# One store in ten of an attention gradient, cut into 120 and 8 partitions

## The chip, the cores and the metric

The kernel runs on one core of one Trainium2 chip. The metric is the device time of one execution in microseconds (us). Three executions of the kernel before took 1323.01, 1326.78 and 1328.87 us; the median is 1326.78.

## The reference

One query attends to 8192 keys, for 2 x 32 = 64 heads of 128 elements, all in bf16. The outputs are the attention's result and the gradients with respect to q, k and v, given the gradient of the result:

```
scores = einsum("bhqd,bhkd->bhqk", q, k) * D**-0.5     # B, H, Sq, Sk, D = 2, 32, 1, 8192, 128
p      = softmax(scores)
out    = einsum("bhqk,bhkd->bhqd", p, v)
# returned: out, and the gradients dq, dk, dv for a given grad_out
```

For each head, k and v (2 MB each) have to be read once, and dk and dv (2 MB each) have to be written once. Every row of dv is the softmax weight of that key times grad_out, and every row of dk is the gradient of that key's score times q. So 537 MB pass between the main memory and the chip, against a few thousand bytes for all else.

## The kernel before, in words

**Tiling.** The 8192 rows of a head are spread over the 128 partitions of the on-chip memory, 64 rows (NT) a partition, so that one partition holds 16 KB that lie in one piece in the main memory. A head's k is one tile kt (128 x 64 x 128), its v one tile vt. There are five buffers of each (UNITS). A load is one DMA of 2 MB, issued on SP's queue (line 103). Transfers of 128 partitions run on sixteen DMA engines, eight partitions to an engine, and each engine reports its own end of the transfer.

**Work on one head.** TensorE turns blocks of kt and vt (line 112, `transposes`), ScalarE or VectorE bring them out of PSUM (lines 119 and 117), and TensorE multiplies them with q and grad_out (line 135, `products`). Then follow the row maximum, the exponentials, the sums and the weights (`row_max` to `weights`). TensorE sums rows for out and dq (line 240, `weighted_rows`). At last VectorE writes the gradients over the loaded tiles themselves (line 270, `outer`): dv over vt, dk over kt. `store` (line 278) sends such a tile to the main memory, one DMA of 2 MB, also on SP's queue. With w = 0 it stores dv out of vt, with w = 1 dk out of kt. The last head alone is stored in halves.

**Order.** The order of all instructions is written out by hand. In step h of the main loop (line 304 and after) the transposes and products of head h are interleaved, in eight parts j, with the weighted rows, the gradients and the stores of head h-1. At the end of step h, load(h+3) is issued (line 343 is its call), into the buffers that head h-2 had; so it waits until both stores of head h-2 have landed. Since loads and stores go out on one queue, in order, whatever waits on SP holds up all that is behind it. Each DMA takes the next of eight semaphores in turn, and first waits for the DMA that had it before.

The lines that matter in what follows: 103 (loads), 112 (transposes), 270 (gradients), 278 (stores), 343 (the call of `load` in the loop).

Of the kernel before, what the change touches and what calls it, by code (L numbers as in the profile page):

```python
# [15 lines left out]
HC = CH // 2  # L16
QG = 4
OG = 4
UNITS = 5


@with_exitstack
def kernel(
# [11 lines left out]
    nc = tc.nc  # L35
    B, H, Sq, D = q.shape
    Sk = k.shape[2]
    P = nc.NUM_PARTITIONS
# [3 lines left out]
    assert NT * P == Sk and NT == 4 * CH and BH <= P and BH % QG == 0  # L42
    assert BH % OG == 0 and OG * 8 == 32
    NS = 2 * NT // CH
# [9 lines left out]

    pick = const.tile([P, 4, 2, OG], F32)
    idv = ident_f[:].rearrange("p (g w k j) -> p g j w k", g=4, w=2, k=OG)
    nc.vector.tensor_copy(out=pick[:], in_=idv[:, 0])
    for g in range(1, 4):
# [6 lines left out]

    kvp = ctx.enter_context(tc.tile_pool(name="kv", bufs=UNITS))
    evp = ctx.enter_context(tc.tile_pool(name="ev", bufs=5))
# [8 lines left out]
    dk_v = out_2.rearrange("b h (p n) d -> (b h) p n d", n=NT)  # L76
    dv_v = out_3.rearrange("b h (p n) d -> (b h) p n d", n=NT)
# [8 lines left out]
    wz = [  # L86
        [const.tile([P, NT // 4, 32], BF16, name=f"wz{w}{k}") for k in range(OG)]
        for w in range(2)
# [5 lines left out]
    heads = [Head() for _ in range(BH)]  # L94

    def load(h):
        x = heads[h]
        x.kv = [
            kvp.tile([P, NT, D], BF16, name="kt", tag="kt"),
            kvp.tile([P, NT, D], BF16, name="vt", tag="vt"),  # L100
        ]
        for dst, src in zip(x.kv, (k_v, v_v)):
            nc.sync.dma_start(out=dst[:], in_=src[h])  # L103
# [79 lines left out]
    def to_weights(h, w, src):  # L183
        k = h % OG
        nc.vector.tensor_copy(  # L185
            out=wz[w][k][:, :, 16 * w + 4 * k : 16 * w + 4 * k + 4],
            in_=src[:].rearrange("p (m j) -> p m j", j=4),
        )
# [44 lines left out]
    def weighted_rows(h, w, chunks):  # L233


        rows, k = heads[h].kv[1 - w], h % OG
        for c in chunks:
# [37 lines left out]
        )  # L275

    def store(h, w, a=0, b=NT):
        nc.sync.dma_start(out=(dv_v, dk_v)[w][h][:, a:b, :], in_=heads[h].kv[1 - w][:, a:b, :])  # L278

    def outer_and_store(h, w, i):  # L280

        outer(h, w, i)
        if h == BH - 1:
            if i % 2:
                store(h, w, (i - 1) * CH, (i + 1) * CH)
        elif i == NT // CH - 1:
            store(h, w)
# [13 lines left out]
    with tc.manual_schedule():  # L301
        for h in range(min(UNITS, BH)):
            load(h)
        for h in range(BH + 1):
# [4 lines left out]
            for j in range(NS):  # L309
# [31 lines left out]
                if j == 7:  # L341
                    if x and UNITS <= h + 3 < BH:
                        load(h + 3)
# [38 lines left out]
```

## Time and profile before

| What | Value |
|---|---|
| Median of three runs | 1326.78 us |
| The profiled execution: its time, its span | 1328.14 us, 1326.3 us |
| Bytes read from and written to main memory | 268.47 MB and 268.47 MB |
| 16 KB packets on SP's queue | 32512, of which the usual one takes 0.611 us |
| Granted TensorE clock, mean | 0.89 |

The span goes from the first instruction to the last. The page of the profile gives the busy time of each compute engine, then the span in forty equal slices with the mean busy share of the sixteen DMA engines (in tenths) and the GB/s that they moved, then the DMA queues with the time that their packets took as a share of sixteen engines' span, and last the DMA issues by line, with the median time from the issue to the landing, which is the last of the sixteen engines' reports. Where a view gives waits, it names who waited for whom, the total, how often, and the longest.

### The profile page before, as it was taken

What the parts mean: (1) busy time and instruction counts of PE and PEld (TensorE: products, weight loads), DVE (VectorE), ACT (ScalarE), POOL (GpSimd) and SP (SyncE); (2) the same over time, 40 slices, a digit from 0 to 9 for tenths busy, and PEclk for the clock granted to TensorE, in tenths of its full rate; (3) what the DMA queues carried; (4) which work ended last, traced back from release to release, by engine and by line L of the source; (5) the groups of instructions that cost most, each with busy time, mean ns of one, the idle gap of its engine ahead of it and who ended that gap; (6) DMA issues with size and microseconds to landing.
All of it is one profiled execution on the core that took longest, in us unless ns stands there. A gap on an engine that the chain in (4) does not pass through costs nothing.

```text
span 1326.3 us, 42070 instructions
## 1 busy us (share of the span) xinstructions
PE 1108.8 (84%) x18948; PEld 909.2 (69%) x18948; DVE 887.3 (67%) x1511; ACT 906.7 (68%) x1043; POOL 4.8 (0%) x16
## 2 busy tenths in 40 slices
PE   5999898898788887888879878798888888898883
PEld 5777777776676766766767667676766676676762
DVE  2887777676666766767657666575766666676664
ACT  5877787776766766767677676676766676676662
POOL 1000000000000000000000000000000000000000
PEclk9999999988988989989799888987988888888886
DMA  9999999999999999999999999999999999999985
GB/s 396 422 427 426 428 426 428 427 427 429 426 426 419 421 413 417 419 412 415 412 410 405 406 403 400 405 405 401 400 397 409 395 406 403 397 401 392 410 371 242
DMA packets 37652, 539.64 MB, mean 407 GB/s; under 512 B 4448, under 2 KB 4448, under 8 KB 4448
## 3 DMA queue, kind: packets, MB, share of 16 engines
q1 hardware_dynamic: 37152, 536.89, 98.2%
q8 instruction: 148, 2.42, 0.6%
q14 instruction: 32, 0.26, 0.0%
q10 hardware_dynamic: 320, 0.07, 0.0%
HBM read 268.47 MB, written 268.47 MB: 405 GB/s over the span
## 4 chain that ended last, share of the span: by engine, by line
DMA 63%; PE 21%; ACT 8%; DVE 4%; issue 1%; SPq 1%; ACTq 0%; DVEq 0%
DMA out_dram<-kt 36%; DMA kt<-in_k_dram 27%; PE tp L112 13%; ACT ev L119 8%; PE acc L240 5%; DVE ev L117 3%; PE sm L135 2%; DMA nat<-in_grad_out_dram 1%; PE dp L205 1%; DVE kt L270 1%; PE dp L135 1%; SPq L103 0%; SPq L278 0%; PE sm L169 0%; DVE vt L270 0%
## 5 line engine op out<-in xcount | busy, mean ns | idle before, releaser
L119 ACT CAST ev<-tp 128x1024 bf16<-128x1024 f32 x896 | 879.2, 1026 | 379.3 <-PE tp L112 364.4
L112 PE MATMUL tp<-ident_bf,kt 128*128 128x128 bf16 x4096 | 379.9, 247 | 119.2 <-DMA kt<-in_k_dram 115.1
L112 PEld LDWEIGHTS <-kt 128*128 128x128 bf16 x4096 | 280.2, 110 | 256.0 <-issue 133.8
L117 DVE CAST ev<-tp 128x1024 bf16<-128x1024 f32 x128 | 156.7, 1224 | 298.5 <-PE tp L112 293.5
L112 PE MATMUL tp<-ident_bf,vt 128*128 128x128 bf16 x4096 | 313.4, 219 | 48.2 <-ACT ev L119 38.0
L135 PEld LDWEIGHTS <-ev 128*128 128x128 bf16 x8192 | 333.0, 100 | 2.2 <-issue 0.2
L112 PEld LDWEIGHTS <-vt 128*128 128x128 bf16 x4096 | 259.1, 98 | 81.6 <-issue 73.1
L270 DVE TENSOR_TENSOR kt<-qd,dS 128x2048 bf16<-128x2048 bf16 x256 | 310.0, 1212 | 0.0
L270 DVE TENSOR_TENSOR vt<-qd,P 128x2048 bf16<-128x2048 bf16 x256 | 295.8, 1217 | 0.0
L135 PE MATMUL dp<-doT_all,ev 128*128 128x1 bf16 x4096 | 180.3, 165 | 0.1
L135 PE MATMUL sm<-qT_all,ev 128*128 128x1 bf16 x4096 | 178.0, 164 | 0.0
L240 PE MATMUL acc<-vt,wz 128*32 128x512 bf16 x1024 | 127.8, 489 | 4.7 <-DVE wz L185 4.5
L240 PE MATMUL acc<-kt,wz 128*32 128x512 bf16 x1024 | 106.1, 407 | 0.5 <-DVE wz L185 0.5
L240 PEld LDWEIGHTS <-wz 128*32 128x32 bf16 x2048 | 53.7, 95 | 16.3 <-DVE wz L185 6.8
L159 DVE TENSOR_REDUCE mp<-sm 128x1 f32<-128x64 f32 x64 | 14.4, 225 | 55.1 <-PE sm L135 55.1
L205 PE MATMUL dp<-ld,ones_f 128*128 128x2 f32 x128 | 27.8, 287 | 10.4 <-DVE ld L192 9.5
L205 PEld LDWEIGHTS dp<-ld,ones_f 128*128 128x128 f32 x128 | 23.3, 228 | 17.8 <-DVE ld L192 17.5
L210 DVE RECIPROCAL rl_all<-dp 128x1 f32<-128x1 f32 x64 | 10.7, 168 | 34.7 <-PE dp L205 34.7
L153 ACT CAST qd<-pb 128x1024 bf16<-128x1024 f32 x16 | 16.2, 1012 | 12.3 <-PE pb L145 12.3
L169 PE MATMUL sm<-gm,ones_f 1*128 1x1 f32 x128 | 24.2, 256 | 0.0
L169 PEld LDWEIGHTS sm<-gm,ones_f 1*128 1x128 f32 x128 | 18.7, 182 | 6.6
L174 ACT ACTIVATE E_f<-sm,negm 128x64 f32<-128x64 f32 x64 | 23.1, 361 | 0.0
(40 smaller groups left out, 263.2 us busy)
## 6 DMA issues: line engine op xcount, KB each, us to landing
kt<-in_k_dram SPq DMA_DIRECT2D x64, 2048.0 KB, 25.4
vt<-in_v_dram SPq DMA_DIRECT2D x64, 2048.0 KB, 30.2
out_dram<-vt SPq DMA_DIRECT2D x63, 2048.0 KB, 34.8
out_dram<-kt SPq DMA_DIRECT2D x63, 2048.0 KB, 39.5
out_dram<-vt SPq DMA_DIRECT2D x2, 1024.0 KB, 12.0
out_dram<-kt SPq DMA_DIRECT2D x2, 1024.0 KB, 12.1
out_dram<-rows ACTq DMA_DIRECT2D x2, 16.0 KB, 5.8
nat<-in_q_dram ACTq DMA_DIRECT2D x1, 16.0 KB, 8.1
```

The source lines that it names most:

```text
L112: nc.tensor.matmul(tp[:, i, :], lhsT=x.kv[w][:, n, :], rhs=ident_bf[:], start=True, stop=True)
L117: nc.vector.tensor_copy(out=ev[:], in_=tp[:])
L119: nc.scalar.copy(out=ev[:], in_=tp[:])
L135: nc.tensor.matmul((x.dp if w else x.sm)[:, n : n + 1], lhsT=ev[:, i, :], rhs=col, start=True, stop=True,)
L153: nc.scalar.copy(out=qd[:], in_=pb[:])
L159: nc.vector.reduce_max(out=x.mp[:], in_=x.sm[:, 0:NT], axis=AX.X)
L169: nc.tensor.matmul(mb, lhsT=ones_f[0:1, :], rhs=x.gm[:], start=True, stop=True)
L174: nc.scalar.activation(out=x.E[:], in_=x.sm[:, 0:NT], func=ACT.Exp, bias=negm[:], scale=scale, accum_out=x.ld[:, 0:1],)
L205: nc.tensor.matmul(x.lsum, lhsT=ones_f[:], rhs=x.ld[:], start=True, stop=True)
L210: nc.vector.reciprocal(out=rl, in_=x.lsum[:, 0:1])
L240: nc.tensor.matmul(acc[32 * g : 32 * g + 32, :], lhsT=wz[w][k][:, n // 4, :], rhs=rows[:, n : n + 4, :].rearrange("p n d -> p (n d)"), sta ...
L270: nc.vector.tensor_tensor(out=x.kv[1 - w][:, n : n + CH, :].rearrange("p n (d t) -> p n d t", t=2), in0=row.unsqueeze(1).to_broadcast([P, ...
```

## The change

In one call of `store` out of ten, the 128 partitions go as two DMAs: partitions 0 to 119, which is eight partitions for each of fifteen DMA engines, and partitions 120 to 127, one for each of the first eight. Counting stores as 2h + w, the ones chosen are 9, 19, ... 119, twelve of 128, and all of them are stores of dk (w = 1, heads 4, 9, ... 59). The same bytes are stored in the same places. Nothing else is changed; the order of the work stays as it was.

```diff
+FEW = 120
+SKIP = 10
 UNITS = 5
...
     def store(h, w, a=0, b=NT):
-        nc.sync.dma_start(out=(dv_v, dk_v)[w][h][:, a:b, :], in_=heads[h].kv[1 - w][:, a:b, :])
+        cuts = (0, FEW, P) if (2 * h + w) % SKIP == SKIP - 1 else (0, P)
+        for lo, hi in zip(cuts, cuts[1:]):
+            nc.sync.dma_start(
+                out=(dv_v, dk_v)[w][h][lo:hi, a:b, :], in_=heads[h].kv[1 - w][lo:hi, a:b, :]
+            )
```

## The prediction

> **What bounds the kernel now.** I read the totals first. The span is 1326.3 us, the execution itself 1328.14 us (1.84 us lie around the span), and the median of the three runs is 1326.78 us, so a sum made against this execution is lowered by 1.36 us to stand beside the median.
>
> ```profile
> span 1326.3 us, 42070 instructions
> PE 1108.8 (84%) x18948; PEld 909.2 (69%) x18948; DVE 887.3 (67%) x1511; ACT 906.7 (68%) x1043; POOL 4.8 (0%) x16
> ...
> DMA  9999999999999999999999999999999999999985
> GB/s 396 422 427 426 428 426 428 427 427 429 426 426 419 421 413 417 419 412 415 412 410 405 406 403 400 405 405 401 400 397 409 395 406 403 397 401 392 410 371 242
> ...
> q1 hardware_dynamic: 37152, 536.89, 98.2%
> q8 instruction: 148, 2.42, 0.6%
> ```
>
> No compute engine is full; the DMA engines are, in every slice but the last two. Yet what they move falls from 427 to about 400 GB/s while their busy share stays full. So "busy" does not mean "at full rate", and next I asked for the stretches before and after that fall.
>
> ```profile
> 60.00:400.00 340.00, 298.57 (x5362) 245.71 (x5360) 250.01 (x426) 256.10 (x296) 0.00 (x0) 0.95 1.01 427
> 800.00:1260.00 460.00, 392.46 (x6494) 321.81 (x6494) 302.92 (x518) 310.80 (x357) 0.00 (x0) 0.85 1.00 401
> ```
>
> Columns are length, PE, PEld, DVE, ACT, POOL, granted clock, DMA share, GB/s. One head moves 8 MB (two loads, two stores): 19.7 us at 427 GB/s, 20.9 at 401. PE's work for a head is 17.3 us in the first stretch and about 17.8 in the second, so PE is not the limit in either. Then the waits of SP's queue:
>
> ```profile
> SPq L103 <- DMA out_dram<-kt: 943.2, 55, 19.5
> SPq L278 <- DVE vt L270: 136.9, 14, 22.1
> ```
>
> A load (line 103) waits until the last store of the head that held its buffers has landed. The DMA issues say how long that is:
>
> ```profile
> kt<-in_k_dram SPq DMA_DIRECT2D x64, 2048.0 KB, 25.4
> vt<-in_v_dram SPq DMA_DIRECT2D x64, 2048.0 KB, 30.2
> out_dram<-vt SPq DMA_DIRECT2D x63, 2048.0 KB, 34.8
> out_dram<-kt SPq DMA_DIRECT2D x63, 2048.0 KB, 39.5
> ```
>
> A transfer alone needs about 5 us; the last store of a head lands 39.5 us after its issue. Who is late? The trace has sixteen completion events for each transfer, one from each DMA engine. For some dk stores, in us from the span's start:
>
> ```
> head  issued    first     8th      15th     16th    16th-15th
>   1     63.51    71.68    72.67    73.70    73.94    0.2
>  14    299.89   324.48   330.39   332.28   339.36    7.1
>  30    627.74   648.74   650.83   652.35   667.21   14.9
>  56   1172.61  1193.32  1194.28  1196.17  1212.74   16.6
> ```
>
> **One DMA engine is late.** Fifteen end within 3 us of each other, the sixteenth 17 us behind, and each next load is issued less than 0.1 us after that sixteenth event. Between 70 and 400 us, before its lag is full, the mean time from one transfer to the next is, ranked by engine: five at 4.87 us, two at 4.90, eight at 4.96 to 4.97 (4.965 below), one at 5.108. In stores the late one needs 5.37 us against 4.93 for the others, in loads 4.86, no more than they. Once it is 18 us behind the first of the others, its lag stands still and the other fifteen slow down, in their loads alone: 4.93 us a load early, 5.55 after 800 us. The late engine sets the pace; the others queue behind a buffer that only it still holds. Extra bytes are not the reason: in the last 8 us it works alone and a 16 KB row (two of 8 KB) takes the usual 0.61 us.
>
> **The change, part by part.** The stores with (2h+w) mod 10 = 9 are twelve: the dk stores of heads 4, 9, ... 59.
>
> *Removed:* if the sixteenth engine (the one that a 120-partition transfer on fifteen leaves out) is the late one, it skips 8 rows in each of the twelve: 12 x 5.37 = 64.4 us of its work. From the tenth transfer (which ends at 52.3 us for the median engine) there are 246 transfers of 2 MB left, counting four halves as two: it had 246 x 5.108 = 1256.6 us and keeps 1192, as little as the five fastest (246 x 4.87 = 1198). It stops being late.
>
> *Added:* one row of 16 KB on each of eight engines, twelve times: a packet took 0.611 us and starts 4 ns before its forerunner's end, so 12 x 0.607 = 7.3 us on each.
>
> *Late next:* the eight engines at 4.965: 52.3 + 246 x 4.965 = 1273.7 us, and with 7.3 more where they are among the eight that take the odd rows, 1281.0. The last instructions follow the last big landing by about 1 us (1325.37 in a span of 1326.3), so 1282; 1.84 around the span makes 1284 in this execution's terms, 1282.5 beside the median. I add 1.5 us for the late stage's loss below, of which I expect a little: **1284 us**, 3.2% less.
>
> *The end:* from the last load's landing (1284.57) compute needs until 1314, then a store 4 us. That is 34 us, and the DMA work left after that load, 8 transfers of 4.965, is 40 us: compute stays hidden, by 6 us.
>
> *Issue:* twelve more DMA instructions on SP's queue, at 0.42 us each (the median dk store). Behind one stands the next store or load, which after 800 us waits some 19 us a head anyway; uncovered it would be 5 us in all. Loads that take the slot now wait for both parts; the small one is queued behind the large one and needs one packet, so at most 0.6 us after it.
>
> *Not shown by the trace:* a transfer of 120 or of 8 partitions. Bounds: the rows dealt evenly over fifteen engines, as now (0); or, as the worst, 15 rows on each of eight engines, 15 x 0.61 = 9.2 us against 4.93, 12 x 4.2 = 51 us more. I take 0, the 128-row transfer being the nearest row. The slowness in stores may belong to rows rather than to the engine (0.06 us a packet); then eight engines share it, and 12 x 0.06 = 0.7 us is the price.
>
> *The late stage:* after 800 us the late engine's v loads took 5.43 us instead of 4.87, which its rows don't explain. If that has to do with the lag, it comes only once the eight are 18 us behind the five (0.1 us a transfer: after some 180), 16 heads x 0.55 = 9 us. If it has to do with time or with the clock (0.95, then 0.85), 18 heads at 0.17 and 25 at 0.55 make 17 us; with both, 1309. Below: were the mean of the fifteen (4.93) to count, 246 x 0.035 = 9 us less, and 7.3 less if the eight slower ones are not the eight that take the odd rows: 1266. Own range of the forecast: 1266 to 1309.
>
> The trace doesn't number its engines, and the row that bears on which one is late is only that there is exactly one. [...]
>
> **The rivals.**
>
> 1. *The late engine is one of the first eight* (slower). It keeps all its rows and gets twelve more: 12 x 0.61 to 0.67 = 7.3 to 8.1 us, paid in full since it is the pace: 1334 to 1335, range 1331 to 1340. It decides from the first split store, and the lag of the sixteenth event stays at 17 us. For it: nothing numbers the engines, and the late one was, as far as it can be followed back, first to finish the very first load. Against: after 60 us no interval of the late engine shows the 0.9 us of an instruction packet (148 of them), which about ten engines do show; it is set apart from the many.
>
> 2. *The late engine is the ninth to fifteenth, or its lag is not what binds* (no change): 1322 to 1332. For the second half: the clock falls in the same stage as the GB/s. Against: the others lose time in loads alone, right behind the sixteenth event.
>
> 3. *The 120 rows are dealt otherwise* (slower): up to the 51 us above, 1335 to 1378.
>
> 4. *PE binds*: 64.5 heads x 17.8 = 1148 us, below the forecast; it could add only waits, within the forecast's range.
>
> **How the numbers follow.** Forecast 0.74, rival 1 0.10, rival 2 0.11, rival 3 0.05. A difference under 0.5% (6.6 us) can't be told from none here. Faster 0.74, same 0.11, slower 0.15; that the late engine is the one left out is my judgement, which the trace supports only so far: it stands apart from the ten with instruction packets, so it is one of six, and a fault of one engine alone fits an end of the row better than its middle. The range is 1266 to 1333: the forecast's own, rival 2, and the lower edge of rival 1, which leaves out under 0.2.
>
> **What would show it.** Right: GB/s near 425 to the last slices; the 16th event within some 10 us of the 15th and no longer one fixed straggler; dk stores landing sooner than 39.5 us; SP's wait for out_dram<-kt well below 943 us. The number of 16 KB packets stays 32512. Wrong: the straggler stays 17 us behind (rivals 1 and 2), twelve stores last 9 us (rival 3), or the sixteen land together and the GB/s still fall to 400, which would mean that time or clock, not one engine, made the fall.

## The result, and the profile after

The changed kernel took 1394.08 us (median of four executions, 1390.18 to 1402.47) against 1326.78 before: 1.0519 times as long, with a 95% interval of 1.0465 to 1.0573. The forecast was 1284, the range 1266 to 1333. The profiled execution took 1392.71 us, its span is 1390.9.

The page of the changed kernel, span and DMA engines (share in tenths, then GB/s, in 40 slices):

```profile
span 1390.9 us, 42077 instructions
...
DMA  9999999999999999999999999999999989999985
GB/s 397 421 427 414 420 426 413 424 426 410 421 423 391 380 409 386 382 401 377 384 397 380 384 386 375 353 390 398 336 386 405 360 352 395 357 368 390 385 341 245
...
q1 hardware_dynamic: 37236, 536.89, 96.2%
```

The GB/s fall further than before, and in dents: a low slice every three, the distance of the split stores. Bytes are unchanged; the 84 more packets are completion events (12 x (15 + 8 - 16)). So the 120 partitions did go on fifteen engines and the eight on eight. No run numbers the engines or shows an order of them: "the first eight" can only be a name for the eight that took the small part, and "the sixteenth" one for the engine that had none of the large part. By stage (length, PE, PEld, DVE, ACT, POOL, clock, DMA share, GB/s):

```profile
60.00:400.00 340.00, 292.64 (x5248) 241.06 (x5245) 243.94 (x417) 249.86 (x289) 0.00 (x0) 0.94 1.00 420
800.00:1260.00 460.00, 364.93 (x5996) 299.06 (x5994) 278.50 (x475) 285.64 (x329) 0.00 (x0) 0.83 0.96 374
```

427 became 420, 401 became 374, and the DMA share hardly shows it (1.01 and 1.00 before, 1.00 and 0.96 now). Around one split store, in stretches of 5 us, with the fourteen faster of its fifteen engines at it from about 861 to 871 us:

```profile
855.00:860.00 5.00, 5.00 (x94) 3.84 (x93) 4.03 (x4) 4.12 (x5) 0.00 (x0) 0.91 0.93 393
860.00:865.00 5.00, 4.57 (x91) 4.18 (x90) 3.90 (x6) 5.00 (x8) 0.00 (x0) 1.00 0.98 360
865.00:870.00 5.00, 1.23 (x29) 1.07 (x26) 1.39 (x3) 1.72 (x2) 0.00 (x0) 0.96 0.81 262
870.00:875.00 5.00, 3.26 (x40) 2.51 (x40) 0.48 (x1) 1.01 (x1) 0.00 (x0) 0.50 1.02 423
875.00:880.00 5.00, 5.00 (x86) 4.02 (x82) 4.25 (x12) 3.21 (x4) 0.00 (x0) 0.86 1.02 321
```

The deepest dent, 262, is at the split store itself. (Stretches of 5 us vary before as well, from 351 to 423 between 855 and 900 us; what made the 321 was not looked into.) SP's waits (total, times, longest) in the changed kernel:

```profile
SPq L105 <- DMA out_dram<-kt: 960.8, 63, 19.9
SPq L284 <- DVE vt L272: 109.1, 13, 21.2
SPq L284 <- DVE kt L272: 74.6, 28, 7.2
SPq L284 <- DMA kt<-in_k_dram: 46.8, 21, 4.5
```

Loads still wait for a dk store. The last wait was 6.3 us, twice, before. Now the small store takes the semaphore of a k load that, from the third split store on, has not landed yet.

**The straggler is still there.** Completion events of the store of v's gradient before a split store, of its two parts, and of the next load, in us from the span's start:

```
                issued   first     8th    next to last   last
dv store        516.89  533.43   534.15      542.63     552.11
dk, 120 part.   517.38  538.29   541.46      549.18     560.46
dk, 8 part.     520.76  539.76                549.79     561.09
next k load     536.64  543.83   546.72      554.90     565.92
```

The engine that is last in the large part is also last in the small one, 0.63 us later, and so it is in all twelve (0.60 to 1.09 us). It was not the engine left out: it is one of the eight that take the small part. And its share of the large part took 8.35 us, not 5.37; in the nine splits after 400 us, 7.3 to 9.95 (8.2 on average).

### The profile page after: what moved, and what is told of

The parts are those of the page before. It is cut to its first block, busy times and chain, and to the rows that moved or that the text cites. A ratio compares the mean times of both kernels' runs of the same rounds, so it can differ in the third digit from the quotient of the medians.

```text
span 1390.9 us, 42077 instructions
## 1 busy us (share of the span) xinstructions
PE 1121.3 (81%) x18948; PEld 920.8 (66%) x18948; DVE 887.6 (64%) x1511; ACT 906.7 (65%) x1043; POOL 4.8 (0%) x16
## 4 chain that ended last, share of the span: by engine, by line
DMA 72%; PE 16%; ACT 7%; DVE 3%; issue 1%; SPq 0%; ACTq 0%; DVEq 0%
DMA kt<-in_k_dram 36%; DMA out_dram<-kt 36%; PE tp L114 9%; ACT ev L121 6%; PE acc L242 4%; DVE ev L119 2%; PE sm L137 1%; DMA nat<-in_grad_out_dram 1%; PE dp L207 1%; DVE kt L272 0%; PE dp L137 0%; DVE vt L272 0%; PE sm L165 0%; ACT E_f L176 0%; PE c L260 0%
## 5 line engine op out<-in xcount | busy, mean ns | idle before, releaser
L114 PE MATMUL tp<-ident_bf,kt 128*128 128x128 bf16 x4096 | 392.1, 252 | 174.7 <-DMA kt<-in_k_dram 171.0
L114 PEld LDWEIGHTS <-kt 128*128 128x128 bf16 x4096 | 289.7, 113 | 315.7 <-DMA kt<-in_k_dram 178.0
L242 PE MATMUL acc<-vt,wz 128*32 128x512 bf16 x1024 | 131.3, 503 | 4.0 <-DVE wz L187 4.0
L207 PEld LDWEIGHTS dp<-ld,ones_f 128*128 128x128 f32 x128 | 26.2, 256 | 11.3 <-DVE ld L194 10.4
```

Of the source, the lines that this page charges most:

```text
L114: nc.tensor.matmul(tp[:, i, :], lhsT=x.kv[w][:, n, :], rhs=ident_bf[:], start=True, stop=True)
L207: nc.tensor.matmul(x.lsum, lhsT=ones_f[:], rhs=x.ld[:], start=True, stop=True)
L242: nc.tensor.matmul(acc[32 * g : 32 * g + 32, :], lhsT=wz[w][k][:, n // 4, :], rhs=rows[:, n : n + 4, :].rearrange("p n d -> p (n d)"), sta ...
```

## Experiments

Theory A: the partitions of a cut store are dealt to the engines otherwise, and engines then get in each other's way. Theory B: the late engine is one of the eight that take the small part and pays for its twelve extra rows, no more. Theory C: one more DMA in the queue costs the time.

### The same number of DMAs, every engine with its own partitions

```diff
-        cuts = (0, FEW, P) if (2 * h + w) % SKIP == SKIP - 1 else (0, P)
+        cuts = (a, NT // 2, b) if (2 * h + w) % 10 == 9 else (a, b)
...
+                out=...[:, lo:hi, :], in_=heads[h].kv[1 - w][:, lo:hi, :]
```

> The same twelve stores go as two DMAs, but cut along each partition's rows (two halves of 8 KB for all 128 partitions), so that every DMA engine keeps its own eight partitions. Theory A (the partitions are dealt to the engines otherwise in a 120-partition store, and engines then get in each other's way): no change, 1322 to 1332 us. Theory B (the late engine is one of the first eight and gets twelve rows more, that alone): no change. Theory C (one more DMA in the queue, its semaphore slot and its issue on SP, cost the time): near the changed kernel's 1394.

Measured: 1329.01 us, 1.0013 times before (0.9996 to 1.0030). SP's waits in it:

```profile
SPq L280 <- DMA kt<-in_k_dram: 65.4, 22, 4.5
```

The new wait for a semaphore is there in full, and costs nothing. Theory C falls.

### Two halves of 64 partitions

```diff
-        cuts = (0, FEW, P) if (2 * h + w) % SKIP == SKIP - 1 else (0, P)
+        cuts = (0, 64, P) if (2 * h + w) % 10 == 9 else (0, P)
```

> The same twelve stores go as partitions 0 to 63 and 64 to 127, so each of sixteen engines still has eight rows of 16 KB in all, but of other partitions. Theory A: a row that shares its way with another engine's takes 1.2 us instead of 0.61 to 0.67, so a store takes the late engine about 9.8 us instead of 5.4: 12 x 4.4 = 53 us more, 1360 to 1395. Theory B: no change, 1322 to 1332, as no engine gets more rows. Theory C: as the changed kernel, 1394.

Measured: 1361.07 us, 1.0256 times (1.0206 to 1.0306). No engine has more rows, and it costs 33 us: theory A, though less than its 53. The late engine's two halves mostly took 2.7 and 3.5 to 5.3 us instead of 5.4 together (one pair early on 2.7 and 2.7, another 4.2 and 3.5).

### The large part alone

```diff
-        cuts = (0, FEW, P) if (2 * h + w) % SKIP == SKIP - 1 else (0, P)
+        cuts = (0, 120) if (2 * h + w) % 10 == 9 else (0, P)
```

> The twelve stores go as partitions 0 to 119 alone; partitions 120 to 127 of these twelve heads' dk are not stored (24 rows of 16 KB each fewer on no engine but the sixteenth). Theory A: the late engine still needs some 8.2 us for such a store: 12 x 2.8 = 34 us more at least, 1355 to 1390. Theory B: 1322 to 1332, as the late engine has its eight rows and no more. Theory C: 1322 to 1332, as no DMA is added.

(The 24 rows named there are a slip: it is 12 x 8 = 96.) Measured: 1352.5 us in one execution and 1375.5 to 1384.1 in three, the profiled one 1379.48. They spread too far for an interval; the one at 1352.5 is 24 us above before, and only that much is sure. The late engine, with its eight rows and no more, took 7.0 to 9.4 us for such a store after 300 us, in the profiled execution, one of the long ones. How much of the loss comes with the large part is told better by the next run.

### The small part alone

```diff
         nc.sync.dma_start(out=(dv_v, dk_v)[w][h][:, a:b, :], in_=...)
+        if (2 * h + w) % 10 == 9:
+            nc.sync.dma_start(out=dk_v[BH - 1][120:P], in_=heads[h].kv[0][120:P])
```

> The twelve stores go whole, as before, and each is followed by an extra store of partitions 120 to 127 (to the place of the last head's rows, which are stored over later), so the first eight engines have the twelve extra rows of the change and all else is dealt as before. Theory A and B: 12 x 0.61 to 0.67 = 7.3 to 8.1 us more if the late engine is one of the first eight, 1332 to 1340; no change if it is not. Theory C: near 1394.

Measured: 1338.94 us, 1.0093 times (1.0062 to 1.0123), 11 us for 8 expected. The late engine's event in each small store came 0.64 to 0.69 us after the end of its whole store. Rival 1 of the prediction, with its price, is real; it is a sixth of what the change cost. This run and the change both send a small part after each of the twelve stores; they differ in the large one, whole here and of 120 partitions there (and in the place that the small one goes to). So most of the loss, 67 - 11 = 56 us, comes with the large part.

### The way out of the on-chip memory, by itself

The kernel stores one tile in eleven kinds of cuts:

```diff
+    phases = ((0, 128, 1, 10), (0, 120, 1, 10), (0, 64, 1, 10), (64, 128, 1, 10), (0, 32, 1, 12),
+              (0, 8, 1, 12), (0, 32, 4, 12), (0, 28, 4, 12), (64, 96, 4, 12), (0, 112, 1, 8), (0, 96, 1, 8))
+    for i, (lo, hi, step, times) in enumerate(phases):
+        nc.sync.dma_start(out=src[:], in_=k_v[i])
+        for _ in range(times):
+            t, h = next(at)
+            nc.sync.dma_start(out=t[h][lo:hi:step], in_=src[lo:hi:step])
```

> Computes nothing of the reference: it only stores partitions of one loaded tile again and again, a kind of cut at a time, with a load between the kinds that waits for all that went before (each row of 16 KB; then three kinds of loads). [...] Besides: a late engine among the first eight shows as one that needs 0.67 us a row; if it is missing with seven partitions (every fourth from 0 to 24) and there with eight, it is the eighth.

From one transfer's completion to the next, median engine, us: 128 partitions 4.86; 0 to 63, 5.09; 64 to 127, 5.08; 0 to 31, 2.57; 0 to 7, 2.57 (the first come 0.4 to 0.9 apart); 0, 4, ... 28, seven of these, and 64, 68, ... 92, 0.61 each. By the last engine's event, the first store of 120 ends 12.0 us after its issue (10.4 for 128 partitions), the next three 7.84, 6.72 and 5.50 us after the one before; then the engines have drifted apart, by 8 us, and it is 4.9. With 112 partitions it swings between 4.9 and 8.9 after the first, with 96 between 4.5 and 5.9. The same in GB/s, for 128 partitions, for stores of 120 early and late, for each half, for 32 and for eight neighbours (this last stretch reaches into the load that follows) (length, POOL, clock, DMA share, GB/s):

```profile
18.10:62.10 44.00, 0.00 (x0) 1.00 1.00 430
84.50:99.00 14.50, 0.00 (x0) 1.00 0.93 308
104.50:129.00 24.50, 0.00 (x0) 1.00 0.95 405
151.00:196.00 45.00, 0.00 (x0) 1.00 0.99 206
216.00:262.00 46.00, 0.00 (x0) 1.00 1.00 209
278.20:306.00 27.80, 0.00 (x0) 1.00 0.97 200
334.90:355.00 20.10, 0.00 (x0) 1.00 0.54 64
```

Sixteen engines on half the partitions move half the bytes in the same time, with a DMA share of 0.99. The packets say it themselves: one of 16 KB took 0.61 us in the median with 128 partitions, 1.27 with 64, twice as long, as if engines met two and two; and 2.54 with eight neighbours, four times as long, as if eight engines met four and four. Every fourth partition, at 0.61, and they don't meet. With 0.61 us for every row, 64 partitions would have taken 2.4 us, 32 of them 1.2, and eight 0.61. So theory A holds, in that engines slow each other in a cut store. Where they meet is not shown: in every run here partition p goes to the p-th 16 KB of a head, so the runs don't tell whether it is at the partitions or at the places in the main memory. The prediction took 0 for this.

No engine is late here, in stores of 128: the sixteen end within 0.9 us of each other, all ten times.

### Quarters, and loads

```diff
-        cuts = (0, FEW, P) if (2 * h + w) % SKIP == SKIP - 1 else (0, P)
+        cuts = (0, 32, 64, 96, P) if (2 * h + w) % 10 == 9 else (0, P)
```

> The twelve stores go as four DMAs of 32 partitions, two rows on each of sixteen engines: still eight rows for each engine. [...] Rival (what counts is one more DMA with fewer partitions): three times the halves' cost, about 1428.

Measured: 1362.98 us, 1.0267 times (1.0232 to 1.0303), as much as two halves. The rival falls: it isn't the number of cuts.

```diff
         for w, (dst, src) in enumerate(zip(x.kv, (k_v, v_v))):
-            nc.sync.dma_start(out=dst[:], in_=src[h])
+            cuts = (0, 64, P) if (2 * h + w) % 10 == 9 else (0, P)
+            for lo, hi in zip(cuts, cuts[1:]):
+                nc.sync.dma_start(out=dst[lo:hi], in_=src[h][lo:hi])
```

> Twelve loads of v (heads 4, 9, ... 59) go as partitions 0 to 63 and 64 to 127; all stores are whole as before. If engines meet on the way into the on-chip memory as they do on the way out, about what the halved stores cost, 1350 to 1365; if only on the way out, 1323 to 1332.

Measured: 1377.44 us, 1.0382 times (1.0348 to 1.0416), more than the halved stores and than expected. The GB/s show each of the twelve:

```profile
GB/s 397 370 426 429 374 427 427 369 424 426 385 389 419 360 408 415 369 388 423 391 362 416 416 330 420 415 339 421 419 332 410 414 328 416 417 350 402 409 394 249
```

Half of the partitions are no faster on the way in, too: the run of stores alone, which ends in loads of partitions 0 to 63, took 5.0 us for each of these.

### Which engine is late

```diff
+        if w and h % 2 and h < BH - 1:
+            nc.sync.dma_start(out=dk_v[BH - 1][126:P], in_=heads[h].kv[0][126:P])
```

> All stores are whole; after the dk store of every second head (31 of them) partitions 126 and 127 are stored once more (to the place of the last head's rows, which are stored over later), as a transfer of two rows, one on each of two engines, the lowest two if the fifteen and the eight of the change were the lowest. [...] If the late engine is one of the first two: 31 x 0.67 = 21 us more, 1346 to 1354, and the last of the two events comes with the late engine's. If it is one of the third to eighth: 1324 to 1332, as the first two have 60 or 35 us to spare.

Measured: 1326.75 us, 0.9975 times (0.9953 to 0.9997). The last of the two events came 16 to 19 us before the late engine's in the second half of the run. So it is not one of these two. In the quarters, the late engine took 1.34 and 1.36 us for the first and the second part, and 1.9 to 2.6 us for the third and the fourth. Whom it meets there is not shown, and may also depend on what the others, 18 us ahead, are doing.

With partitions 0, 4, ... 24 (seven), and with 28 as well (eight), in the same place:

```diff
+            nc.sync.dma_start(out=dk_v[BH - 1][0:28:4], in_=heads[h].kv[0][0:28:4])
```

> All stores are whole; after the dk store of every second head (31 of them) the seven partitions 0, 4, ... 24 are stored once more (to the place of the last head's rows, which are stored over later), one row on each of seven engines, each by its own way. If the late engine is the third to seventh: 31 x 0.67 = 21 us more, 1346 to 1354. If it is the eighth: no change, 1323 to 1333, as the seven have time to spare.

> As with seven, and partition 28 too: eight rows on the first eight engines, each by its own way. The late engine is among the eight, so 31 x 0.67 = 21 us more, 1346 to 1354, whichever it is. If seven cost nothing and eight cost this, it is the eighth.

Measured: 1359.39 us, 1.0257 times (1.0214 to 1.0300), and 1360.85, 1.0272 (1.0230 to 1.0314). In both, the last event comes 0.6 to 0.7 us after the end of the late engine's store, from the second small store on. So the late engine is in transfers of seven and not in those of two. (The two kinds ran on different chips; that the late engine has the same place on both was taken for granted.) That it costs 33 us and not 21 is read off in the table below. Which of the seven it is, no run shows.

### An attempt to spare it

```diff
+        c = 3 * NT // 4
+        nc.sync.dma_start(out=out[:, :c, :], in_=src[:, :c, :])
+        for lo, hi in ((0, 119), (119, 126), (126, P)):
+            nc.sync.dma_start(out=out[lo:hi, c:, :], in_=src[lo:hi, c:, :])
```

> [...]

Measured: 1364.15 us, 1.0289 times (1.0247 to 1.0331), 38 us more than before. The last quarter of the rows went in parts of 119, 7 and 2 partitions, to spare an engine that a transfer of eight takes and one of seven doesn't. The two runs before place the late engine in the transfers of seven, so it is not the one that this was made for. On how many engines 119 partitions go is not shown.

### Without compute

```diff
+        for h in range(3):
+            load(h)
+        for h in range(BH):
+            for w in range(2):
+                nc.sync.dma_start(out=(dv_v, dk_v)[w][h], in_=tiles[h][1 - w][:])
+            if h + 3 < BH:
+                load(h + 3)
```

> Computes nothing of the reference: the same 128 loads and 128 stores of 2 MB on the same five pairs of buffers, without any work between them. If the late engine is slow in stores because loads and stores run at the same time, it is late here too (5.37 us a store, 17 us behind at the end, and some 1290 to 1310 us in all); if it is slow because of the compute engines or their instruction packets, the sixteen end together, at 4.87 us a transfer, 256 x 4.87 + 10 = 1257 us.

Measured: 1255.16 us (one execution).

```profile
GB/s 393 426 429 429 428 429 428 430 429 433 430 432 431 431 432 429 435 429 433 430 432 431 431 431 430 434 429 433 429 432 430 431 431 430 434 429 434 429 432 375
```

426 to 435 GB/s in all slices but the first and the last; the sixteen stay within 4.5 us, and the last to end needs 4.84 us a dk store and 4.91 a dv store. It is one execution, but the chip is that of the run with partitions 126 and 127, where one engine was 18 us late. So here the fall of the GB/s, and the slow stores of one engine, came only beside the compute. (The 148 instruction packets went with it, so the run doesn't tell the two apart.)

## Why the prediction was wrong

**What bounds the kernel: right.** One engine sets the pace: 62 extra rows on two other engines cost nothing (1326.75 us), 31 rows each on seven that include it cost 33 us. (The prediction's "Fifteen end within 3 us of each other" holds, about, from head 30 on; its own table has 7.8 us at head 14.) What each kernel ends later than before adds up on that engine by itself; the table shows where, from 100 us on (us more than before, profiled executions; the stores that are cut or added, where a whole one counts 5.37, the others against their sums in before):

```
                   cut or added  other dk  v loads  k loads  sum   last landing
rows cut                0.4        0.4      1.6     -1.6     0.8      -0.7
small part alone        8.0        0.0      2.9     -0.9     9.9       8.6
halves of 64           18.5        5.6     15.6      1.1    40.8      39.7
large part alone       23.3       13.2     11.1      3.6    51.2      51.4
the change             36.3        9.3     15.1      4.2    64.9      64.5
seven rows, 31 times   20.0        0.8     15.2     -0.8    35.1      33.8
eight rows, 31 times   19.8        0.9     12.5     -0.8    32.4      31.9
```

(dv stores, left out, are within 1.5 us.) Of the 36.3 us of the change, 27.6 are the large parts and 8.7 the small ones. That the two parts run alone make up the whole is not shown: the large part's row is of one of its long executions (1379.48 us, another took 1352.5).

**"If the sixteenth engine ... is the late one": wrong.** That step carried the whole gain: 64.4 us off the late engine, where the runs show 64.9 us more on it. The text itself said that the trace doesn't number its engines and took 0.74 for it; that a fault fits an end of the row better than its middle was a guess. No run shows an order of the engines, or the 64.4 us; the completion events show the late engine in the part of 120 partitions and in the part of 8, in all twelve. The case for one of the eight that take the small part was in the text, and left at 0.10. No run here spared the late engine, so what the sum says of the fifteen others, 1284, stays untested.

**"I take 0, the 128-row transfer being the nearest row": wrong, and the larger error.** The bound above it was 51 us and stood in the text as rival 3, at 0.05; the runs show about that much, 56 us between the small part alone and the change, by another mechanism. The rows were dealt evenly, eight to an engine (120 partitions in a row settle at the 4.9 us of eight rows), and still took the late engine 8.2 instead of 5.4 us. (Engines slow each other in such stores: the run of stores alone moved 308 GB/s in the first ones of 120 partitions, against 430 with 128.) That is 56 of the 67 us lost; the gain not had is 43. A cut is paid three times: when the late engine runs its share (the first column), when the others, some 18 us ahead, run theirs and hold up a whole store of the late engine's (the second), and in its v loads (the third, whose cause is open). The second shows in which stores are slow: in the change, from head 14 on, the late engine's dk stores one head before a cut one took 6.68 us on average and up to 8.8, the other whole ones 5.34 to 5.37 on average.

**Added rows: right in size, on the wrong engine's account.** 12 x 0.607 = 7.3 us was to be hidden on eight engines with time to spare. One of the eight had none: 8.0 us on it, 11 us in the median.

**Issue and semaphores: right.** Cutting along the rows cost 0.13%, at most 0.3%. **PE, and the end: right**; neither decided. **Rival 1** had the direction and its mechanism, at 1334 to 1335; the rest of 1394 is the dealing, which no rival had in a form that every engine keeps its eight rows.

**The late stage: open.** At 4.87 us each, the late engine's v loads are 15 us too long in before, 17 and 18 with the rows cut and with the small part alone, and 26 to 31 in the other runs of the table. In those with seven and eight extra rows, the rows themselves take 20 us, as expected, and the v loads most of the rest of their 33. Why the v loads, and why its stores are slow only beside compute, no run tells. Nor was it settled whom it meets: in the halved stores its second half was the slow one, 3.5 to 5.3 us against 2.7.

## What to carry to other kernels

Before rows are moved off one of several parallel units, find out which unit is the slow one: a small extra transfer whose completion events can be counted tells in one run whether it is among the units that the transfer uses. A transfer over another set of partitions is not the same transfer with fewer rows; here 128 partitions moved 430 GB/s and 64 moved 206, both with a DMA share of 0.99 or more. Price a cut along the partitions by such a run, and cut along the rows where only the count matters.

## What the runs showed of the hardware that was not expected

A full busy share of the DMA engines says little of their rate: 1.00 went with 430 GB/s for 128 partitions, and 0.99 with 206 for 64. Stores of 120 partitions in a row slow each other only until the engines have drifted apart (7.84, 6.72, 5.50, then 4.9 us); one such store among others, as in the change, took the late engine 7.3 to 9.95 us each time after 300 us. One engine of sixteen needed 5.37 us for a store beside compute, and 4.84 to 4.91 was what the last one needed without it.
